# Three pairs of heads per block of products with v, and two feature blocks per bank of turned expert tokens

## The chip, the cores and the metric

The kernel runs on one core of one Trainium2 chip. The metric is the device time of one execution in microseconds (us), the median of several runs. Beside the timed runs one execution was profiled; its rows are what the prediction reads.

## The reference

Three layers follow each other, all in 32-bit floats.

- Attention with talking heads: 4 batches, 12 heads, 448 positions, 64 columns per head. The scores q k^T / 8 of all heads are mixed by a 12 x 12 matrix (w_pre), a softmax over the keys follows, its result is mixed over the heads by a second matrix (w_post), and then multiplied with v.
- A dense layer over the 1792 tokens: x w_in (768 to 2048), ELU, w_out (2048 to 768).
- A layer of 8 experts: each token goes to the expert with the largest gate logit, passes w1 (768 to 1024), ReLU and w2 (1024 to 768), and is scaled by its gate.

## The kernel before

**Attention.** Each batch's 448 query positions are cut into chunks of 120, 120, 120 and 88 (16 chunks, cc = 0 to 15). A chunk is cut into groups of 20 positions (6, 6, 6 and 5 groups), and one group passes through in one slot of a hand-written order. Its steps are:

- `qk` (L222, tile p_qk): scores of one pair of heads for a whole chunk; `qk_out` (L229 on DVE, L231 on ACT) copies them to the scratch tile st.
- `relayout` (L239): DMAs issued by POOL bring one group's 12 heads side by side (tile sp).
- `premix` (L248, p_pre): the first mix over heads; `rowmax` (L253, DVE) takes its extremes, and `expo` (L259, ACT) the exponentials with their sums (tile pt).
- `scale` (L265 to L269, DVE) puts 1/sum into the second mixing matrix; `postmix` (L278, p_post) does the second mix, transposed. Its PSUM tile, two banks, has one buffer (tag "post"). `mt_out` (L296, ACT) copies it to mt, which collects a chunk's groups.
- `av` (L322, p_av): the products with v for some pairs of heads of a whole chunk, into one PSUM bank (tag "av", one buffer); `av_out` (L329, DVE) copies it to xc, and L330, a DMA on SP's queue, writes that to the scratch array xscr.

The order is fixed beforehand: every call is entered by `at(slot, order, fn)` or `half(y, ...)` with y in half slots, and all entries are issued sorted by slot and order number. Each engine's queue works in that order. `S0[cc]` is the slot of chunk cc's first group. Group x has its premix at slot x, its exponentials at x + 1, its postmix at x + 2.5 and its mt_out at x + 3. In an integer slot the order is qk, premix, scale, qk_out (DVE), rowmax, expo (of the group before), mt_out; in a half slot it is qk_out (ACT), av if one is due, postmix. `turns` gives the slots of av. `room` picks, for work that can wait (av_out, and the steps that decode weights), the half slot with the least planned load of an engine.

The last two chunks have all their av blocks at one slot, in several banks.

**Dense layer.** `moe1` starts as attention ends and reads xscr; its code isn't touched.

**Experts.** `moe2` takes the experts in the order PLACES, with 256, 288, 288 and then five times 256 token rows. For each of them 8 "h" jobs (first product, L1218 with tile p_h) are followed by 8 "z" jobs (L1203, p_z, where the rows are a multiple of 128) or 6 "y" jobs (L1218, p_y). The next expert's rows are gathered by DMA (L1165) and turned by `trans(p, ks)` during the z or y jobs of the one before: PE transposes (L90) into a bank p_t (tag "t", two buffers), an ACT copy to the high part xgh (L1181) and a DVE subtraction for the low part xgl (L1182), one feature block of 128 at each of the jobs 0 to 5. The same stretch splits the weights into high and low parts (L110 on ACT, L112 on DVE).

Of the kernel before, what the change touches and what calls it, by code (L numbers as in the profile page):

```python
# [5 lines left out]
F32 = mybir.dt.float32  # L6
# [3 lines left out]
AF = mybir.ActivationFunctionType  # L10
ALU = mybir.AluOpType
# [6 lines left out]
NE, FE = 8, 1024  # L18
NTOK = NB * S
JC, NJ = 112, 4  # L20
KD = DM // 128
# [23 lines left out]
def blocks(n):  # L45
    return [min(128, n - o) for o in range(0, n, 128)]
# [41 lines left out]
def transpose(nc, out, in_, ident):  # L88

    nc.tensor.transpose(out, in_, ident)  # L90
# [10 lines left out]
def after(tc, ins, writes):  # L101
    for w in writes:
        tc.add_manual_dep(ins.ins, w.ins.name, mybir.DependencyInfo(mybir.DependencyClass.Sync, mybir.DependencyReason.DATA),
                          reason="rows of any scatter")
# [42 lines left out]
NCH = NB * 4  # L147
S0 = [0]
# [6 lines left out]
def attention(tc, pools, at, q, k, v, kron_pre, kron_post, dec_jobs, xscr):  # L155
# [3 lines left out]
    nc = tc.nc  # L159
    mm = nc.tensor.matmul  # L160
    sb = pools.open("a_sb", "right")
    early = pools.open("a_early", "left")
    ps = pools.open("a_ps", "right", PSUM)
    ps_qk = pools.open("a_psqk", "left", PSUM)
# [12 lines left out]
    ks, qs, qp, st, sp, pre, mxs, pt, sms, kpt, pst, mt, vt, avp, draw, dsteps = ({} for _ in range(16))  # L177
# [127 lines left out]
    def av(cc, a):  # L305

        n = CHUNKS[cc % 4]
        if cc == NCH - 1:

            p = ps.tile([128, 512], F32, name="p_av", tag="pre", bufs=3)  # L310
        elif cc == NCH - 2 and a:
            if a == 1:
                avp["two"] = [ps_qk.tile([128, 512], F32, name="p_av", tag=f"qk{e}") for e in range(2)]
            p = avp["two"][a - 1]
        else:
            p = ps_qk.tile([128, 512], F32, name="p_av", tag="av")
        p = avp[cc, a] = p[:, :256].rearrange("p (u c) -> p u c", c=128)
        for u in range(2):
            for j in range(4):
                for e in range(2):  # L320
                    h = 4 * a + 2 * u + e
                    mm(p[64 * e:64 * e + 64, u, :n], lhsT=vt[cc // 4][:, j, h, :], rhs=mt[cc][:, j * H + h, :n],  # L322
                       start=(j == 0), stop=(j == 3))

    def av_out(cc, a):
        b, c = divmod(cc, 4)
        n, o = CHUNKS[c], sum(CHUNKS[:c])
        x = sb.tile([128, 2, 120], F32, name="xc", tag="xc", bufs=3)
        nc.vector.tensor_copy(x[:, :, :n], avp.pop((cc, a))[:, :, :n])  # L329
        nc.sync.dma_start(xscr[b][:, 2 * a:2 * a + 2, o:o + n], x[:, :, :n])  # L330

    def dec_load(n, hf):
        draw[n, hf] = dec.load(dec_jobs[n][0], hf)
# [12 lines left out]
    def half(y, order, fn, *args):  # L346
        at(y / 2, order, fn, *args)

    def take(y, **cost):
        for e, c in cost.items():  # L350
            use[e, y] = use.get((e, y), 0) + c
        return y

    def room(lo, hi, **cost):
        return take(min(range(lo, max(lo, hi) + 1), key=lambda y: max(use.get((e, y), 0) + c for e, c in cost.items())), **cost)

    def when(cc, u):

        if cc == 0:
            return 2 * ((2 * u + 1) * 10 // 12 - 13)  # L360
        lo, hi = S0[cc - 1] - 3, S0[cc] - 3
        return 2 * lo + u * (2 * hi - 2 * lo) // 6

    for cc in range(NCH):
        z = S0[cc]
        for u in range(6):
            y = when(cc, u)
# [5 lines left out]
        for g, (T, nr) in enumerate(UNITS[cc % 4]):  # L373
            x = z + g
# [7 lines left out]
            at(x + LAG + 1, 26, mt_out, cc, g)  # L382
            take(2 * x, dve=185, act=200)
            take(2 * x + 1, act=60)
    turns = {(cc, a): 2 * (S0[cc + 1] + (2 if cc >= NCH - 2 else 3 + 2 * a)) + 1 for cc in range(NCH) for a in range(3)}
    for (cc, a), y in turns.items():
        half(y, 9, av, cc, a)
        soon = cc >= NCH - 2 or y + 2 in turns.values()
        half(y if soon else room(y + 1, y + 2, dve=35), 36, av_out, cc, a)
    for b in range(NB):  # L390
        for j in range(4):
            at(S0[4 * b] - 6 + j if b else 1 + j, 4, load_v, b, j)
# [5 lines left out]
    N = 2 * len(dec_jobs)  # L398
    first, free = 3, [0, 0]
    for i in range(N):  # L400
        n, hf = divmod(i, 2)
# [5 lines left out]
        y = room(y + 1, y + 2, act=61)  # L407
        half(y, 36, dec_step, n, hf, 1)
        y = room(y, y + 1, dve=57)
        half(y, 42, dec_step, n, hf, 3)  # L410
        y = room(y + 1, y + 2, dve=101)
# [696 lines left out]
def moe2(tc, pools, w1, w2, ident_d, x2rows, R, out):  # L1108
    nc = tc.nc
    mm = nc.tensor.matmul  # L1110
    P = {}
# [9 lines left out]
    def size(p):  # L1121
        return SIZES[PLACES[p]]
# [12 lines left out]
    def load(n):  # L1135
        if n < NJB:
            p, s, i = jobs[n]
            e = R["of"][PLACES[p]]
            if s == "h":
                t = P["w1"].tile([128, DM], F32, name="w1raw", tag="w1raw", bufs=6)  # L1140
                ins = nc.sync.dma_start(t, w1f[bass.ds(e * (NFE * 128) + i * 128, 128), :])
            elif s == "y":
                t = P["sb"].tile([128, NFE, 128], F32, name="w2raw", tag="w2raw", bufs=5)
                src = w2f[bass.ds(e * FE, FE), i * 128:(i + 1) * 128]
                ins = nc.sync.dma_start(t, src.rearrange("(f p) c -> p f c", p=128))
            else:
                t = P["sb"].tile([128, DM], F32, name="w2raw", tag="w2raw", bufs=5)
                ins = nc.sync.dma_start(t, w2f[bass.ds(e * FE + i * 128, 128), :])
            raws[n] = t
            return ins  # L1150

    def prep(n):
        if n < NJB:
            p, s, i = jobs[n]
            if s == "h":
                ws[n] = split(nc, P["w1"], raws.pop(n), "w1", [128, DM], 3)
            else:
                ws[n] = split(nc, P["sb"], raws.pop(n), "w2", [128, NFE, 128] if s == "y" else [128, DM], 3)

    def gather(p):  # L1160
        bl = blocks(size(p))
        g = xg[p] = P["w1"].tile([128, len(bl), DR], F32, name="xg", tag="xg")
        at = R["tok"][:, PLACES[p]] if p else R["tok1"][:, 0]
        gate[p] = P["w1"].tile([128, len(bl)], F32, name="gate", tag="gate", bufs=2)
        return [nc.gpsimd.indirect_dma_start(g[:n, j, :], None, x2rows, IndirectOffsetOnAxis(at[:n, j:j + 1], 0))  # L1165
                for j, n in enumerate(bl)]

    def trans(p, ks):
        sb = P["sb"]
        N = size(p)  # L1170
        if 0 in ks:
            xgs[p] = (sb.tile([128, KD, N], F32R, name="xgh", tag="xgh"),
                      sb.tile([128, KD, N], F32R, name="xgl", tag="xgl"))
        g, (hi, lo) = xg[p], xgs[p]

        ts = {kk: bank("t") if p == 0 and kk > 1 else P["t"].tile([128, 512], F32, name="p_t", tag="t", bufs=2) for kk in ks}
        for j, n in enumerate(blocks(N)):
            for kk in ks:
                transpose(nc, ts[kk][:, j * 128:j * 128 + n], g[:n, j, kk * 128:(kk + 1) * 128], P["ident"][:n, :n])
        for kk in ks:  # L1180
            nc.scalar.activation(hi[:, kk, :], ts[kk][:, :N], AF.Copy)  # L1181
            nc.vector.tensor_tensor(lo[:, kk, :], ts[kk][:, :N], hi[:, kk, :].bitcast(F32), ALU.subtract)  # L1182
        if KD - 1 in ks:
            for j, n in enumerate(blocks(N)):
                nc.scalar.activation(gate[p][:n, j:j + 1], g[:n, j, DM:], AF.Copy)

    def bank(nm):
        return P["ps"].tile([128, 512], F32, name=f"p_{nm}", tag="y", bufs=4)
# [69 lines left out]
    def rest():  # L1258
        P["sb"] = pools.open("e_sb", "left")
        P["ps"] = pools.open("e_ps", "right", PSUM)  # L1260
        P["sep"] = P["sb"].tile([1, 1], F32, name="sep")
        load(0)
        for n in range(1, 9):

            after(tc, load(n), P["got"][:1] if n == 1 else [])
        prep(0)
        trans(0, range(KD))
        prep(1)
        prep(2)
        for n in range(NJB + 1):  # L1270
            if n < NJB:
                p, s, i = jobs[n]
                if s == "h" and i == 1 and p + 1 < NE:
                    gather(p + 1)
                load(n + 9)
                run(n)
                prep(n + 3)
                if s != "h" and i < KD and p + 1 < NE:
                    trans(p + 1, [i])
            if n >= 1:  # L1280
                finish(n - 1)
        pools.close("e_sb", "e_ps", "e_pst", "e_w1", "m_x2")
# [165 lines left out]
```

## Time and profile before

| | us |
|---|---|
| median of 3 runs | 1209.93 (1209.03 to 1212.42) |
| the profiled execution | 1198.01 |
| its span, from first to last instruction | 1196.2 |
| PE (matmul) busy | 1148.1 |
| DVE busy | 766.2 |
| ACT busy | 683.5 |
| POOL busy | 295.4 |

Busy times are unions of an engine's instructions; ends of matmuls are modelled, so that neighbours overlap in the records and the pace of PE is read from start to start. In the timeline a row is a run of equal instructions of one line: start, duration, engine, line, operation, output and input, shapes, count. In square brackets stands the engine's idle time before it and what ended it. A pair "x2" of records belongs to one product of 32-bit floats, so a block of 16 products shows as x32. Attention fills the span to about 350 us, the dense layer to about 860, the experts the rest.

### The profile page before, as it was taken

To read this page: it belongs to the slowest core of one execution; us is meant where nothing else is said; L and a number is where in the kernel's file an instruction comes from. 1 tells how busy PE (TensorE), PEld (TensorE's weight loads), DVE (VectorE), ACT (ScalarE), POOL (GpSimd) and SP (SyncE) were. 2 spreads that over 40 slices of the span, in tenths; PEclk is the share of its full clock that TensorE was granted. 3 is DMA by queue.
4 is the path that set the end of the run, shared out by engine and by line. 5 is a ranking of instruction groups with operands and counts; after the bars stand their busy time and mean duration, and the time that the engine had idled before them with its cause. 6 is when DMAs were issued, how large, how long until landed. Compare 5 with 4: busy or idle time off the path is not lost.

```text
span 1196.2 us, 31070 instructions
## 1 busy us (share of the span) xinstructions
PE 1148.1 (96%) x12798; PEld 975.4 (82%) x12798; DVE 766.2 (64%) x1540; ACT 683.5 (57%) x1310; POOL 295.4 (25%) x466
## 2 busy tenths in 40 slices
PE   6999999999988999999999999999989999999995
PEld 1566666666667999999999987989779999999995
DVE  2777876777765878677777656555365655566662
ACT  2877876877875674645555344555434544455552
POOL 3765656656630003020211100000010110111110
PEclk7999999999999999999999999999999999999998
DMA  7698698897664528365573623434166665666651
GB/s 207 185 234 202 184 234 205 204 229 198 175 184 131 150 79 219 119 141 136 146 192 100 154 68 100 133 99 141 46 228 209 217 175 190 203 226 230 203 198 63
DMA packets 116444, 201.47 MB, mean 168 GB/s; under 512 B 45024, under 2 KB 76370, under 8 KB 116292
## 3 DMA queue, kind: packets, MB, share of 16 engines
q1 hardware_dynamic: 78116, 138.01, 37.5%
q0 software_dynamic: 38176, 61.37, 21.4%
q8 instruction: 103, 1.69, 0.6%
q14 instruction: 49, 0.40, 0.1%
HBM read 120.94 MB, written 30.09 MB: 126 GB/s over the span
## 4 chain that ended last, share of the span: by engine, by line
PE 88%; ACT 4%; DVE 3%; DMA 2%; issue 1%; POOL 0%; SPq 0%; POOLq 0%; ACTq 0%; DVEq 0%
PE p_h L520 14%; PE p_o L560 14%; PE p_h L1218 11%; PE p_z L1203 8%; PE p_post L278 7%; PE p_av L322 7%; PE p_pre L248 6%; PE p_qk L222 5%; PE acc L586 5%; PE p_o L520 4%; PE p_y L1218 3%; DMA sp<-st 1%; ACT mt L296 1%; PE p_t L90 1%; PE tp L90 1%
## 5 line engine op out<-in xcount | busy, mean ns | idle before, releaser
L239 POOL DMA_DIRECT2D sp<-st x360 | 208.6, 596 | 129.9 <-PE p_pre L248 59.9
L259 ACT ACTIVATE pt<-p_pre,mx 128x448 f32<-128x448 f32 x180 | 112.8, 635 | 43.2 <-DVE mx L253 43.0
L278 PEld LDWEIGHTS p_post<-kp,pt 60*64 60x64 f32 (+1 forms) x5056 | 88.6, 134 | 44.1 <-ACT mt L296 31.1
L253 DVE TENSOR_REDUCE mx<-p_pre 128x1 f32<-128x448 f32 x180 | 104.1, 619 | 27.3 <-PE p_pre L248 22.7
L296 ACT ACTIVATE mt<-p_post 128x960 f32<-128x960 f32 (+1 forms) x92 | 101.7, 1105 | 34.0 <-PE p_post L278 33.8
L278 PE MATMUL p_post<-kp,pt 60*64 60x60 f32 (+2 forms) x5056 | 108.9, 228 | 10.0 <-issue 4.9
L577 POOL DMA_DIRECT2D x<-part x46 | 41.3, 921 | 294.7 <-ACT part L576 291.7
L1218 PE MATMUL p_h<-xgl,w1h 128*128 128x256 f32 (+1 forms) x384 | 109.3, 285 | 0.6 <-DVE xgl L1182 0.5
L1218 PE MATMUL p_h<-xgh,w1l 128*128 128x256 f32 (+1 forms) x384 | 109.3, 285 | 0.3 <-DVE w1l L112 0.3
L248 PE MATMUL p_pre<-sp,kpre 60*64 60x448 f32 x720 | 105.9, 551 | 3.8 <-DMA sp<-st 3.8
L1218 PE MATMUL p_h<-xgh,w1h 128*128 128x256 f32 (+1 forms) x384 | 109.4, 285 | 0.0
L560 PE MATMUL p_o<-gh,woh 128*128 128x448 f32 x288 | 106.4, 370 | 2.6 <-DVE x L573 2.6
L222 PE MATMUL p_qk<-ks,qs 64*64 64x448 f32 x744 | 100.0, 557 | 9.0 <-ACT st L231 5.1
L560 PE MATMUL p_o<-gl,woh 128*128 128x448 f32 x288 | 105.2, 365 | 0.0
L560 PE MATMUL p_o<-gh,wol 128*128 128x448 f32 x288 | 104.9, 364 | 0.0
L322 PEld LDWEIGHTS p_av<-mt,vt 128*64 128x64 f32 x1536 | 74.6, 138 | 31.6 <-DVE kp L269 12.7
L229 DVE COPY st<-p_qk 128x448 f32<-128x448 f32 x93 | 57.9, 622 | 63.1 <-PE p_qk L222 60.1
L112 DVE TENSOR_TENSOR w2l<-w2raw,w2h 128x768 fp32r<-128x768 f32 (+1 forms) x60 | 60.7, 1012 | 51.7 <-ACT w2h L110 51.7
L540 DVE SCALAR_TENSOR_TENSOR th<-rm,th 128x448 f32<-128x448 f32 x64 | 40.0, 625 | 79.8 <-ACT rm L539 79.8
L1254 POOL DMA_INDIRECT out_dram<-yrow,put x18 | 23.8, 1323 | 252.8 <-ACT w1h L110 86.6
L322 PE MATMUL p_av<-mt,vt 128*64 128x120 f32 (+1 forms) x1536 | 84.3, 264 | 0.5 <-ACT mt L296 0.5
L112 DVE TENSOR_TENSOR w1l<-w1raw,w1h 128x768 fp32r<-128x768 f32 x64 | 60.9, 960 | 28.3 <-ACT w1h L110 25.1
(196 smaller groups left out, 2804.3 us busy)
## 6 DMA issues: line engine op xcount, KB each, us to landing
sp<-st POOLq DMA_DIRECT2D x352, 105.0 KB
w1raw<-in_w_dram SPq DMA_DIRECT2D x64, 384.0 KB, 6.9
w2raw<-in_w_dram SPq DMA_DIRECT2D x48, 384.0 KB, 2.9
x<-part POOLq DMA_DIRECT2D x46, 224.0 KB
raw<-in_w_in_dram SPq DMA_DIRECT2D x13, 768.0 KB, 5.7
raw<-in_w_out_dram SPq DMA_DIRECT2D x13, 768.0 KB, 5.2
wtmp<-wscr SPq DMA_DIRECT2D x19, 384.0 KB, 4.0
wtmp<-oscr SPq DMA_DIRECT2D x19, 384.0 KB, 5.2
```

The costliest lines, as they stand in the source:

```text
L112: nc.vector.tensor_tensor(l, src, a.bitcast(F32), ALU.subtract)
L222: mm(p[e][64 * a:64 * a + 64, :S], lhsT=qq[r, c:c + 64], rhs=kk[r], start=True, stop=True)
L239: nc.gpsimd.dma_start(t[64 * r:64 * r + 12 * T, c], st[cc][f:f + d * (T - 1) + 1:d])
L248: mm(ban[r][64 * c:64 * c + 64, :S], lhsT=kpre[x], rhs=t[x, c, :], start=True, stop=True)
L253: nc.vector.tensor_reduce(mxs[cc, g][:, r:r + 1], pre[cc, g][r][:, :S], AX.X, ALU.min)
L259: nc.scalar.activation(pt[cc, g][:, r], pre[cc, g][r][:, :S], AF.Exp, bias=mxs[cc, g][:, r:r + 1], scale=-1.0, accum_out=sms[cc, g][:, r:r ...
L278: mm(out, lhsT=e[x, r, 64 * s:64 * s + 64], rhs=kp[x, w].rearrange("p w (h i) -> p w h i", i=5)[:, :, :, :T], start=True, stop=True)
L296: nc.scalar.activation(dst, src, AF.Copy)
L322: mm(p[64 * e:64 * e + 64, u, :n], lhsT=vt[cc // 4][:, j, h, :], rhs=mt[cc][:, j * H + h, :n], start=(j == 0), stop=(j == 3))
L520: mm(p[:, :S], lhsT=a[:, c], rhs=m, start=(i == 0), stop=(i == 17))
L560: mm(p[:, :S], lhsT=a[:, c], rhs=m, start=(k == 0), stop=(k == 3 * len(fs) - 1))
L1218: mm(q[:, :N], lhsT=a[:, kk, :], rhs=m[:, kk, :], start=(j == 0), stop=(j == len(seq) - 1))
```

## The change

In `av` and `av_out` a block covers three pairs of heads instead of two, so that a chunk has two blocks (a = 0, 1) instead of three. A block is due at S0[cc + 1] + 3.5 + 3a instead of + 3.5 + 2a; for the last two chunks still all at one slot. The tile xc becomes half as wide again and has two buffers instead of three; the planned load of its copy is 50 instead of 35. In `trans` the feature blocks are taken in sets: of two where two times the rows fit into 512 columns, of one otherwise. A set has one bank, one ACT copy and one DVE subtraction, and is made at the first of the two jobs.

```diff
         elif cc == NCH - 2 and a:
-            if a == 1:
-                avp["two"] = [ps_qk.tile([128, 512], F32, name="p_av", tag=f"qk{e}") for e in range(2)]
-            p = avp["two"][a - 1]
+            p = ps_qk.tile([128, 512], F32, name="p_av", tag="qk0")
         else:
             p = ps_qk.tile([128, 512], F32, name="p_av", tag="av")
-        p = avp[cc, a] = p[:, :256].rearrange("p (u c) -> p u c", c=128)
-        for u in range(2):
+        p = avp[cc, a] = p[:, :384].rearrange("p (u c) -> p u c", c=128)
+        for u in range(3):
             for j in range(4):
                 for e in range(2):
-                    h = 4 * a + 2 * u + e
+                    h = 6 * a + 2 * u + e
...
-        x = sb.tile([128, 2, 120], F32, name="xc", tag="xc", bufs=3)
+        x = sb.tile([128, 3, 120], F32, name="xc", tag="xc", bufs=2)
         nc.vector.tensor_copy(x[:, :, :n], avp.pop((cc, a))[:, :, :n])
-        nc.sync.dma_start(xscr[b][:, 2 * a:2 * a + 2, o:o + n], x[:, :, :n])
+        nc.sync.dma_start(xscr[b][:, 3 * a:3 * a + 3, o:o + n], x[:, :, :n])
...
-    turns = {(cc, a): 2 * (S0[cc + 1] + (2 if cc >= NCH - 2 else 3 + 2 * a)) + 1 for cc in range(NCH) for a in range(3)}
+    turns = {(cc, a): 2 * (S0[cc + 1] + (2 if cc >= NCH - 2 else 3 + 3 * a)) + 1 for cc in range(NCH) for a in range(2)}
...
-        half(y if soon else room(y + 1, y + 2, dve=35), 36, av_out, cc, a)
+        half(y if soon else room(y + 1, y + 2, dve=50), 36, av_out, cc, a)
...
+    def width(p):
+        return 2 if p and 2 * size(p) <= 512 else 1
+
     def trans(p, ks):
...
-        ts = {kk: bank("t") if p == 0 and kk > 1 else P["t"].tile([128, 512], F32, name="p_t", tag="t", bufs=2) for kk in ks}
+        w = width(p)
+        sets = [ks[i:i + w] for i in range(0, len(ks), w)]
+        ts = [bank("t") if p == 0 and i > 1 else P["t"].tile([128, 512], F32, name="p_t", tag="t", bufs=2) for i in range(len(sets))]
+        ts = [t[:, :w * N].rearrange("p (k n) -> p k n", k=w) for t in ts]
         for j, n in enumerate(blocks(N)):
-            for kk in ks:
-                transpose(nc, ts[kk][:, j * 128:j * 128 + n], g[:n, j, kk * 128:(kk + 1) * 128], P["ident"][:n, :n])
-        for kk in ks:
-            nc.scalar.activation(hi[:, kk, :], ts[kk][:, :N], AF.Copy)
-            nc.vector.tensor_tensor(lo[:, kk, :], ts[kk][:, :N], hi[:, kk, :].bitcast(F32), ALU.subtract)
+            for t, kks in zip(ts, sets):
+                for i, kk in enumerate(kks):
+                    transpose(nc, t[:, i, j * 128:j * 128 + n], g[:n, j, kk * 128:(kk + 1) * 128], P["ident"][:n, :n])
+        for t, kks in zip(ts, sets):
+            c = slice(kks[0], kks[-1] + 1)
+            nc.scalar.activation(hi[:, c, :], t, AF.Copy)
+            nc.vector.tensor_tensor(lo[:, c, :], t, hi[:, c, :].bitcast(F32), ALU.subtract)
...
-                if s != "h" and i < KD and p + 1 < NE:
-                    trans(p + 1, [i])
+                if s != "h" and i < KD and p + 1 < NE and i % width(p + 1) == 0:
+                    trans(p + 1, range(i, i + width(p + 1)))
```

## Rows read from the trace of the kernel before

**Rows 1.** The page, part 1: busy us, share of the span, instructions
```profile
PE 1148.1 (96%) x12798; PEld 975.4 (82%) x12798; DVE 766.2 (64%) x1540; ACT 683.5 (57%) x1310; POOL 295.4 (25%) x466
```

**Rows 2.** Windows: us, busy of PE, PEld, DVE, ACT, POOL, clock, DMA, GB/s
```profile
54.00:157.00 103.00, 100.31 (x2480) 68.38 (x2476) 75.64 (x202) 79.21 (x172) 62.27 (x108) 1.00 0.83 204
157.00:346.00 189.00, 183.20 (x4530) 124.02 (x4522) 137.48 (x376) 145.35 (x313) 116.30 (x201) 1.00 0.82 204
...
1080.00:1115.00 35.00, 35.00 (x253) 34.81 (x252) 21.50 (x32) 18.27 (x34) 5.58 (x6) 1.00 0.66 221
```

**Rows 3.** Timeline of PE, two slots of attention: start us, duration us, instructions
```profile
172.62 1.18 PE L278 MATMUL p_post<-kp,pt 60*64 60x60 f32 x56
...
174.33 0.98 PE L248 MATMUL p_pre<-sp,kpre 60*64 60x448 f32 x8
175.09 1.16 PE L278 MATMUL p_post<-kp,pt 60*64 60x60 f32 x56
176.00 1.00 PE L222 MATMUL p_qk<-ks,qs 64*64 64x448 f32 x8
176.75 1.09 PE L248 MATMUL p_pre<-sp,kpre 60*64 60x448 f32 x8
177.77 1.86 PE L322 MATMUL p_av<-mt,vt 128*64 128x120 f32 x32
179.56 1.18 PE L278 MATMUL p_post<-kp,pt 60*64 60x60 f32 x56
```

**Rows 4.** Timeline of ACT and DVE in the same two slots
```profile
173.85 1.14 ACT L296 ACTIVATE mt<-p_post 128x960 f32<-128x960 f32 x1 [1.34 <-PE p_post L278]
...
175.37 1.16 DVE L253 TENSOR_REDUCE mx<-p_pre 128x1 f32<-128x448 f32 x2
...
176.09 0.63 ACT L259 ACTIVATE pt<-p_pre,mx 128x448 f32<-128x448 f32 x1 [0.71 <-DVE mx L253]
...
177.32 1.13 ACT L296 ACTIVATE mt<-p_post 128x960 f32<-128x960 f32 x1
```

**Rows 5.** Attention before the first p_av: a window of five slots, and the timeline
```profile
35.90:50.90 15.00, 13.39 (x360) 7.92 (x360) 13.30 (x36) 14.01 (x32) 12.68 (x23) 1.00 0.67 193
...
40.61 1.13 ACT L296 ACTIVATE mt<-p_post 128x960 f32<-128x960 f32 x1
...
41.79 1.18 PE L278 MATMUL p_post<-kp,pt 60*64 60x60 f32 x56 [0.55 <-ACT mt L296]
...
44.93 1.18 PE L278 MATMUL p_post<-kp,pt 60*64 60x60 f32 x56 [0.46 <-ACT mt L296]
```

**Rows 6.** Timeline: a slot with p_pre ahead of p_qk; one after the last scores
```profile
81.89 1.14 PE L278 MATMUL p_post<-kp,pt 60*64 60x60 f32 x56
...
83.81 1.14 ACT L296 ACTIVATE mt<-p_post 128x960 f32<-128x960 f32 x1
...
333.76 1.18 PE L278 MATMUL p_post<-kp,pt 60*64 60x60 f32 x56 [0.47 <-ACT mt L296]
```

**Rows 7.** The chain that ended last: start us, us; three p_av blocks in a row
```profile
346.13 5.14 PE p_av L322 x96
```

**Rows 8.** Experts and copies: the chain, the timeline, and groups by line and form
```profile
1064.45 2.12 PE p_z L1203 x12
1066.79 2.12 PE p_z L1203 x12
...
1076.12 4.20 PE p_z L1203 x24
...
1011.46 0.39 PE L1218 MATMUL p_h<-xgl,w1h 128*128 128x256 f32 x1 [0.47 <-DVE xgl L1182]
...
L329 DVE COPY xc<-p_av 128x240 f32<-128x240 f32 x36 | 14.4, 400 | 3.7 <-PE p_av L322 3.6
...
L1181 ACT ACTIVATE xgh<-p_t 128x256 fp32r<-128x256 f32 x36 | 12.9, 375 | 4.6 <-PE p_t L90 4.6
L1182 DVE TENSOR_TENSOR xgl<-p_t,xgh 128x256 fp32r<-128x256 f32 x36 | 14.6, 419 | 1.2 <-ACT xgh L1181 1.2
```

## The prediction

> **What bounds the kernel now.** I read the page first: TensorE (PE) is busy 96% of the span [rows 1]. Then the windows view: between 54 and 346 us, the regular part of attention, PE is idle 2.7 of 103 us and 5.8 of 189 us, 8.5 us together, and among the experts not at all [rows 2]. So nothing that ACT or DVE are spared can come out of the time unless PE waits for it; what counts is whether PE gets new waits, and what its own work costs.
>
> The two places that the change touches are read in the timeline. [rows 3] are PE's blocks in two slots of attention, each from its start to the next one's. A slot is p_post, p_qk, p_pre; every second one ends with a block of 32 p_av records. Without p_av it is 172.62 to 175.09, 2.47 us. With it: p_post 0.91, p_qk 0.75, p_pre 1.02, p_av 1.79, together 4.47. Two slots are 6.94. Note that p_pre takes 0.75 when p_post follows and 1.02 when p_av does: changing over to p_av costs PE 0.27 us.
>
> The second thing to see is what the next p_post waits for. Its PSUM tile has one buffer, so it needs the ACT copy mt (L296) of the one before. [rows 4] show that copy twice. After the p_post of 172.62 it runs at 173.85 to 174.99, just in time for the p_post of 175.09. After the p_post of 175.09 it is late: p_pre ran at 174.33 to 175.31, so the row maxima start at 175.37, the first exponential at 176.09, a second follows, and ACT, which works in order, reaches mt at 177.32 and ends it at 178.45, 3.36 us after that p_post began. Today this costs nothing: PE is in the p_av block until 179.56. **The p_av block of every second slot hides a late mt.**
>
> **Part 1: p_av in two blocks per chunk.** The 24 products of three pairs go into one bank (384 of its 512 columns). Products, bytes and packets stay as they are; blocks fall from 48 to 32, with as many DVE copies and SP DMAs.
>
> The due slots matter. Chunk cc has its blocks 3.5 and 6.5 slots after the next chunk's first group, where it had them 3.5, 5.5 and 7.5 after. Chunks have 6, 6, 6 and 5 groups, so for chunks 0 to 13 the blocks stand at 28 slots (9.5, 12.5, 15.5 ... 84.5, 87.5) with 27 gaps: 24 of three slots and 3 of two. Today 41 gaps: 38 of two, 3 of one. **In each gap of three there are two slots in a row without p_av**, a case that [rows 3] don't have.
>
> Price of such a gap. Call the p_post after a block A, the next ones B and C. A to B is 2.47 as today. B to C: everything that decides mt's lateness lies ahead of the block that is taken away, so mt still ends 3.36 after B, and p_post starts some 0.05 later (mt 40.61 to 41.74, p_post 41.79 [rows 5]): 3.41 where 2.47 would do, a wait of 0.94. C to the next A: 0.91 + 0.75 + 1.02 and the larger block. Three blocks in a row, 96 records, took 5.14 [rows 7], so 48 take 2.57 by that and 2.69 as 1.5 times 1.79; I take the middle, 2.63: 5.31. Three slots are 2.47 + 3.41 + 5.31 = 11.19, where today's pace gives 1.5 x 6.94 = 10.41: 0.78 more, the fewer changeovers already taken off (they and the joint block are worth 0.16 to 0.2 a gap).
>
> The trace has a stretch to check it: before slot 9 there are no p_av blocks. There five slots took 15.0 us, 3.0 each, two of them 6.0 against my 5.88, with PE idle 0.55 and 0.46 ahead of p_post for mt [rows 5]. So the wait is real, and comes about once in two slots.
>
> Of the 24 gaps, 3 lie where a five-group chunk turns the order of p_qk and p_pre round. There mt ends earlier: 81.89 to 84.95, 3.06 [rows 6]; against 2.41 of work it is a wait of 0.70, net 0.54. One more lies after the last scores, where PE already waits 0.47 for mt in slots without p_av [rows 6]; I take nothing for it. Sum: 20 x 0.78 + 3 x 0.54 = 17.2 us.
>
> Against this, other waits can shrink: the transfers, ACT and the scratch for the next chunk gain 0.78 us in each three slots. All of PE's other idle time there is 8.5 us [rows 2], which bounds it: between 0 and 8.5. I take 4, since some of it is seen as late ACT and DMA work and some only as issue. **Attention: +13.**
>
> Costed at nothing: the DVE copy L329, 0.40 us for 240 columns [rows 8], which would be some 0.5 for 360 (estimate, a quarter more for half as many columns again) but comes once in three slots instead of once in two; it stands behind the row maxima of its half slot and has three slots until the bank is wanted. Without that cover it would cost 0.1 us 32 times, 3 us. The xc tile has two buffers for three, against copies half again as far apart. The last read of mt comes one slot earlier. SP issues 16 DMAs fewer, and nothing queued behind them is late. Chunks 14 and 15 keep their blocks back to back at the same slot, as now.
>
> **Part 2: expert tokens.** Where two feature blocks fit a bank (256 tokens: five of the eight experts' transfers), 30 pairs of ACT copy and DVE subtraction become 15 of 512 columns. They cost 0.375 and 0.419 us now [rows 8], beside a PE that is busy all 35 us of such an expert [rows 2]: nothing to gain from them, and nothing to lose while an even step (2.34 us) holds a weight split and one larger pair. The transposes keep their number. A step with two takes 2.34 us, without 2.10 (4.20 for two [rows 8]): 0.24. How much of this belongs to the pair and how much to changing over isn't shown; the bounds are nothing and half of it, 15 x 0.12 = 1.8. I take 1.4. The last pair is made one step earlier, which removes the 0.47 us wait on xgl at 1011.46 [rows 8], 0.6 with its restart. **Experts: -2.**
>
> **Sum.** The profiled execution has 1198.0 us (span 1196.2); 17.2 - 4 - 2 = +11 makes it 1209. The median of the runs shown, 1209.93, lies 1% above it, and I put the difference on that: **1221 us**.
>
> **Rivals.**
> Faster: mt isn't late for C. The decision point is 2.41 us after B, when PE could start p_post; mt would have to end there and not at 3.36. For it: ACT has 0.71 us of idle time ahead of those exponentials, and DVE's other work is moved a little. Against: the chain from p_pre over row maximum and two exponentials is already tight (0.06, 0.1 us between its links [rows 4]), and [rows 5] show it late without p_av too. Price: 14 changeovers at 0.27 and some 1.5 of joint blocks, -5, experts -2: 1203. The Trainium skill (TensorEngine Tiling (Array Packing), Key Properties) says that changing the tiling mode drains TensorE, so fewer p_av blocks among 64-row products should mean fewer drains; the 0.27 of [rows 3] agrees, and by that rule alone the time would fall to about this rival's.
> No change: the new waits swallow all the idle time of today: 17.2 - 8.5 - 2 = +7 with my price; with the waits at the recorded 0.5 of [rows 5] less 0.16 instead of 0.78, 24 x 0.34 - 4 - 2 = +2: 1212.
> Slower still: nothing shrinks and the load works (decode steps on ACT, the larger copy on DVE) fall into slot C, where anything on ACT's queue ahead of mt now delays PE: 17.2 + 3 = +20: 1230.
>
> **Chances.** Forecast 0.62; slower still 0.20; no change 0.11; faster 0.07. About 0.3%, 3.6 us, is what a measurement of this kernel can tell from no change. Of the forecast's and the heavier case nearly all lies beyond it: slower 0.83, same 0.10, faster 0.07. The range 1211 to 1230 runs from the no-change case's edge to the heavier one; only the faster rival and some tails stay out.
>
> **What would show it.** Right: in the changed profile p_av blocks of 48 records three slots apart (10.4 us becomes about 11.2); ahead of every third p_post an idle PE that ends on ACT mt, together 15 to 20 us; the sum of p_av's records smaller; no new idle PE among the experts, and the wait at xgl gone. Wrong: 10.4 us from block to block with no wait on mt, or waits on p_av's bank, xc or the transposes' banks.

## The result and the profile after

The changed kernel takes 1222.37 us (median of 6 runs, 1215.92 to 1226.67); the kernel before took 1207.05 us beside it (median of 6 runs, 1202.35 to 1212.42). The ratio is 1.0135, with an interval of 1.0102 to 1.0167: slower by 15.3 us. The profiled execution took 1222.1 us, with a span of 1220.3, and stands at the median; the profiled execution of before, 1198.0, was shorter than every other run of that kernel in this study, so the two spans alone would give 24 us, and more profiles are needed for a fair account (below).

The page of the changed kernel, part 1, columns as in [rows 1]:

```profile
PE 1151.0 (94%) x12798; PEld 981.0 (80%) x12798; DVE 763.5 (63%) x1509; ACT 681.4 (56%) x1295; POOL 294.5 (24%) x466
```

PE has as many instructions and 3 us more of busy time; the span has grown by 24. The new time is idle time of PE. The windows say where (columns as in [rows 2]; the second window ends at the last p_av blocks, the third is one expert):

```profile
54.00:157.00 103.00, 91.92 (x2216) 63.44 (x2212) 68.18 (x180) 71.44 (x155) 56.10 (x99) 0.98 0.75 185
157.00:372.00 215.00, 196.08 (x4790) 134.56 (x4792) 144.23 (x386) 153.50 (x332) 122.32 (x212) 0.98 0.76 189
1098.00:1133.00 35.00, 35.00 (x256) 34.90 (x255) 21.18 (x29) 17.98 (x32) 5.55 (x6) 1.00 0.66 224
```

Attention has 11.1 and 18.9 us of idle PE, 30.0 together, for 8.5 in [rows 2]. The expert has none, as before. One more number differs: the granted clock, 0.98 for 1.00.

**The slots.** The timeline of PE in one gap of three slots, from the p_post after a p_av block (A) over B and C to the next A:

```profile
139.82 1.18 PE L278 MATMUL p_post<-kp,pt 60*64 60x60 f32 x56
...
141.53 0.98 PE L248 MATMUL p_pre<-sp,kpre 60*64 60x448 f32 x8
142.28 1.14 PE L278 MATMUL p_post<-kp,pt 60*64 60x60 f32 x56
143.19 0.98 PE L222 MATMUL p_qk<-ks,qs 64*64 64x448 f32 x8
143.95 1.09 PE L248 MATMUL p_pre<-sp,kpre 60*64 60x448 f32 x8
145.69 1.18 PE L278 MATMUL p_post<-kp,pt 60*64 60x60 f32 x56 [0.66 <-ACT mt L296]
146.65 0.98 PE L222 MATMUL p_qk<-ks,qs 64*64 64x448 f32 x8
147.41 0.97 PE L248 MATMUL p_pre<-sp,kpre 60*64 60x448 f32 x8
148.31 2.68 PE L320 MATMUL p_av<-mt,vt 128*64 128x120 f32 x48
150.92 1.18 PE L278 MATMUL p_post<-kp,pt 60*64 60x60 f32 x56
```

A to B is 2.46, B to C 3.41 (p_pre stands 1.74 ahead of C, where it takes 0.75 ahead of B), C to the next A 5.23: 11.10 in all, and the gaps like it that have no other wait repeat that to 0.03 (10.46, where the block that ends the gap is one of an 88-column chunk). The timeline of ACT in the same gap:

```profile
141.04 1.14 ACT L296 ACTIVATE mt<-p_post 128x960 f32<-128x960 f32 x1 [1.01 <-PE p_post L278]
...
143.28 0.63 ACT L259 ACTIVATE pt<-p_pre,mx 128x448 f32<-128x448 f32 x1 [0.71 <-DVE mx L253]
...
144.52 1.13 ACT L296 ACTIVATE mt<-p_post 128x960 f32<-128x960 f32 x1
```

It is the picture of [rows 4], instruction for instruction: behind B the row maxima, two exponentials, then mt, which ends at 145.65, 3.37 after B. What has changed is PE alone: no p_av block stands there any more, and PE waits. The chain of waits in the same stretch (start us, us, what) runs where it ran over PE before:

```profile
143.28 1.34 ACT pt L259 x4
144.62 1.03 ACT mt L296
...
145.69 1.18 PE p_post L278 x49
```

**PE's waits on "issue".** The waits of PE from 25 to 375 us (total us, times, longest):

```profile
PE p_post L278 <- ACT mt L296: 10.8, 18, 0.7
PE p_post L278 <- issue: 8.8, 6, 2.5
PE p_qk L222 <- issue: 8.2, 3, 3.5
```

In before the first line had 4.8 us, and issue 4.9 in all. So the largest new item under these names isn't the wait that was forecast: 17.0 us end on nothing that the profile names. (The names tell less than the pace. Of the 0.95 that a late C costs, 0.66 is named; the rest stands in the records as a longer p_pre, for the ends of matmuls are modelled.) The longest waits on issue, in the chain of waits of the changed kernel:

```profile
111.76 2.45 issue
...
193.74 2.94 issue
...
284.87 3.49 issue
```

One of them by windows of the changed kernel (busy of PE first, the last three columns are the granted clock, the DMA engines' share and GB/s):

```profile
186.00:190.00 4.00, 4.00 (x93) 3.14 (x89) 2.84 (x10) 2.54 (x6) 1.19 (x2) 1.00 1.01 249
...
194.00:196.70 2.70, 0.02 (x3) 0.03 (x3) 0.35 (x2) 1.27 (x3) 1.18 (x3) 0.85 0.81 218
196.70:198.30 1.60, 1.60 (x11) 0.75 (x14) 0.00 (x0) 0.54 (x1) 0.00 (x0) 0.50 0.91 235
198.30:200.00 1.70, 1.70 (x30) 1.18 (x24) 1.28 (x3) 0.07 (x1) 0.00 (x0) 0.50 1.04 243
```

The DMA engines are full, PE stands still for 2.7, and then its clock is granted at 0.50, which is 1.2 of 2.4 GHz; it is back at full speed some 6 us after the standstill. This happens three times in the profile (at about 114, 196 and 288 us), each time behind one of the long waits above. It isn't in [rows 2], where the clock is 1.00.

**Experts and copies.** The groups by line and form (out<-in xcount | busy us, mean ns | idle before), which answer to [rows 8]:

```profile
L327 DVE COPY xc<-p_av 128x360 f32<-128x360 f32 x24 | 12.5, 522 | 4.2 <-DMA xscr<-xc 2.6 <-PE p_av L320 1.6
...
L1188 DVE TENSOR_TENSOR xgl<-p_t,xgh 128x512 fp32r<-128x512 f32 x15 | 10.3, 685 | 0.0
L1187 ACT ACTIVATE xgh<-p_t 128x512 fp32r<-128x512 f32 x15 | 8.7, 583 | 0.0
```

And the chain of waits through one expert:

```profile
1069.86 16.90 PE p_h L1224 x144
1086.75 2.09 PE p_z L1209 x12
1088.84 0.44 PE p_t L90 x4
1089.28 4.17 PE p_z L1209 x24
...
1104.74 5.28 PE p_h L1224 x45
```

From one p_h to the next it is 34.88 us; in before the same distance was 35.06 (1045.25 to 1080.31). The wait of p_h on xgl [rows 8] is gone. From the first p_h to the last p_z the experts take 296.78 us for 298.16.

### The profile page after: what moved, and what is told of

Its sections match the earlier page's. It is cut to its first block, busy times and chain, and to the rows that moved or that the text cites. A ratio compares the mean times of both kernels' runs of the same rounds, so it can differ in the third digit from the quotient of the medians.

```text
span 1220.3 us, 30980 instructions
## 1 busy us (share of the span) xinstructions
PE 1151.0 (94%) x12798; PEld 981.0 (80%) x12798; DVE 763.5 (63%) x1509; ACT 681.4 (56%) x1295; POOL 294.5 (24%) x466
## 4 chain that ended last, share of the span: by engine, by line
PE 84%; ACT 6%; DVE 4%; DMA 3%; issue 2%; POOL 1%; SPq 0%; ACTq 0%; POOLq 0%; DVEq 0%
PE p_h L518 14%; PE p_o L558 13%; PE p_h L1224 12%; PE p_z L1209 8%; PE p_av L320 7%; PE p_post L278 6%; PE p_qk L222 5%; PE acc L584 5%; PE p_pre L248 5%; PE p_o L518 4%; PE p_y L1224 3%; DMA sp<-st 2%; ACT mt L296 2%; ACT pt L259 2%; DVE mx L253 1%
## 5 line engine op out<-in xcount | busy, mean ns | idle before, releaser
L278 PEld LDWEIGHTS p_post<-kp,pt 60*64 60x64 f32 (+1 forms) x5056 | 92.6, 135 | 67.8 <-ACT mt L296 50.0
L278 PE MATMUL p_post<-kp,pt 60*64 60x60 f32 (+2 forms) x5056 | 112.5, 229 | 24.1 <-ACT mt L296 11.8
L222 PE MATMUL p_qk<-ks,qs 64*64 64x448 f32 x744 | 106.1, 568 | 15.3 <-issue 8.2
L320 PE MATMUL p_av<-mt,vt 128*64 128x120 f32 (+1 forms) x1536 | 81.5, 263 | 0.7 <-ACT mt L296 0.7
L489 ACT ACTIVATE gh<-th 128x448 fp32r<-128x448 f32 x64 | 37.0, 578 | 71.8 <-DVE th L539 71.8
```

The source lines that it names most:

```text
L222: mm(p[e][64 * a:64 * a + 64, :S], lhsT=qq[r, c:c + 64], rhs=kk[r], start=True, stop=True)
L278: mm(out, lhsT=e[x, r, 64 * s:64 * s + 64], rhs=kp[x, w].rearrange("p w (h i) -> p w h i", i=5)[:, :, :, :T], start=True, stop=True)
```

## The experiments

**The two parts alone.** Theory: all of the loss comes from the p_av blocks, and the experts give back a little. Part 1 alone puts back the transposes and copies of before:

```diff
-        w = width(p)
-        sets = [ks[i:i + w] for i in range(0, len(ks), w)]
...
+            nc.scalar.activation(hi[:, kk, :], ts[kk][:, :N], AF.Copy)
+            nc.vector.tensor_tensor(lo[:, kk, :], ts[kk][:, :N], hi[:, kk, :].bitcast(F32), ALU.subtract)
```

> Part 1 alone: p_av in two blocks per chunk, the expert tokens turned as before. Theory (a late mt in every gap of three slots): the slower time stays, some 15 us over the kernel before, ratio 1.012 to 1.016; p_post to p_post goes 2.46, 3.41, 5.2 us; the experts take as long as before, and the 0.47 us wait on xgl is there again. Rival (the two parts add up differently, the experts lose): at most 5 us over the kernel before.

Part 2 alone puts back three blocks of two pairs:

```diff
-        for u in range(3):
+        for u in range(2):
...
-                    h = 6 * a + 2 * u + e
+                    h = 4 * a + 2 * u + e
...
-    turns = {(cc, a): 2 * (S0[cc + 1] + (2 if cc >= NCH - 2 else 3 + 3 * a)) + 1 for cc in range(NCH) for a in range(2)}
+    turns = {(cc, a): 2 * (S0[cc + 1] + (2 if cc >= NCH - 2 else 3 + 2 * a)) + 1 for cc in range(NCH) for a in range(3)}
```

> Part 2 alone: expert tokens in sets of two, p_av as before. Theory: nothing waits for the copies, only transposes and the one wait on xgl give a little: 1 to 2 us less from the end of attention to the end of the program, ratio 0.998 to 1.000, in the total hardly to be told from no change; attention as before, 2.46 and 4.47 us from p_post to p_post. Rival (a share of the slowdown comes from the experts): over 1.003.

Measured, both beside 1204.76 us of before: part 1 alone 1219.33 us, ratio 1.0111 (1.0089 to 1.0133); part 2 alone 1205.42 us, ratio 0.9993 (0.9967 to 1.002). The loss is part 1's. Part 2's gain is too small for the whole time to show it, and is read from the trace: first p_h to last p_z 297.01 us, 1.2 less than before, and in the seven profiles of this study with part 2 and all loads it is 296.6 to 297.2, for 298.0 to 298.7 in the four without part 2.

**Gaps of two and four slots.** If a gap of three costs because its second slot without p_av comes late, the loss should depend on how the slots are dealt out. The second block of a chunk is made due one slot earlier:

```diff
-... else 3 + 3 * a)) + 1 for cc in range(NCH) for a in range(2)}
+... else 3 + 2 * a)) + 1 for cc in range(NCH) for a in range(2)}
```

> The changed kernel with its two blocks per chunk due 3.5 and 5.5 slots after the next chunk's first group, in place of 3.5 and 6.5: gaps of two and four slots by turns, the same blocks. Theory (the wait belongs to the second slot in a row without p_av, and the next one has none, as in the stretch before the first block): no wait in a gap of two, 0.94 us and some 0.2 in a gap of four, so about 0.75 us a chunk less than the changed kernel: some 9 us less, ratio to the kernel before near 1.005. Rival 1 (the size of a block costs, not its place): as the changed kernel, 1.013. Rival 2 (each slot without p_av after the first waits 0.94): 1.013 as well, with a second late slot in every gap of four.

Measured: 1216.62 us, ratio 1.0091 (1.0063 to 1.0118). The timeline of PE in a gap of four slots of this kernel:

```profile
163.13 1.13 PE L278 MATMUL p_post<-kp,pt 60*64 60x60 f32 x56
...
166.54 1.18 PE L278 MATMUL p_post<-kp,pt 60*64 60x60 f32 x56 [0.65 <-ACT mt L296]
...
169.18 1.18 PE L278 MATMUL p_post<-kp,pt 60*64 60x60 f32 x56
```

One slot of 3.41, and the next is 2.64 again: a late mt lets ACT catch up. This gap pays once, like a gap of three, and a gap of two pays nothing. But only four of the ten gaps of four are like it; in the other six the slot after the late one takes 3.0 to 3.9 as well. So the waits weren't halved: 17 slots without p_av have an mt that ends more than 2.95 us after its p_post, for 24, 22 and 23 in the three profiles of the same blocks in gaps of three. Six fewer at 0.69 to 0.95 are 4 to 6 us, and by the ratios about 5 us came back. The expected 9 us didn't, the issue waits remained (11.2 us, one of them 4.60), and the clock fell twice. The direction and the count of late slots speak for the theory.

**Where the wait is made: the late mt on another engine.** In the groups whose mt is late the copy goes to DVE, with scale, row maximum and av_out moved out of its way:

```diff
-        nc.scalar.activation(dst, src, AF.Copy)
+        if S0[cc] + g in late:
+            nc.vector.tensor_copy(dst, src)
+        else:
+            nc.scalar.activation(dst, src, AF.Copy)
...
-            at(x + LAG + 1, 26, mt_out, cc, g)
+            at(*((x + LAG + .5, 11) if x in late else (x + LAG + 1, 26)), mt_out, cc, g)
```

> The changed kernel, but the copy mt of the second group after each block, the one that comes late on ACT behind two exponentials, is made by DVE right after its p_post; in these gaps the scaling of the next group and the copy of p_av are moved out of its way. Theory (the wait is on that copy and its place on ACT alone): mt ends some 2.5 to 2.8 us after its p_post in place of 3.36, p_post to p_post becomes about 2.5 to 2.9 in place of 3.41, 24 times, 12 to 20 us less than the changed kernel: ratio to the kernel before 0.997 to 1.003. Rival 1 (ACT and DVE together are the bound in three slots): the wait only moves to the row maxima or the exponentials, within 5 us of the changed kernel. Rival 2 (PE's waits on issue are what the change added): they stay, 8 us or more over the kernel before.

Measured: 1219.46 us, ratio 1.0104 (1.0082 to 1.0126), which can't be told from the changed kernel's 1.0135. The timeline of this kernel, a gap whose B stood at 149.56:

```profile
151.30 1.19 DVE L297 COPY mt<-p_post 128x960 f32<-128x960 f32 x1
...
152.55 1.18 PE L278 MATMUL p_post<-kp,pt 60*64 60x60 f32 x56
...
153.97 1.15 DVE L253 TENSOR_REDUCE mx<-p_pre 128x1 f32<-128x448 f32 x2
...
154.68 0.63 ACT L259 ACTIVATE pt<-p_pre,mx 128x448 f32<-128x448 f32 x1 [1.95 <-DVE mx L253]
...
155.46 0.98 PE L248 MATMUL p_pre<-sp,kpre 60*64 60x448 f32 x6 [0.29 <-ACT pt L259]
```

C comes 2.99 after B for 3.41, so the place is right. But the row maxima now stand behind mt on DVE, ACT waits 1.95 for them, and the next p_pre waits for the exponentials: what one slot saves the next one loses, and the 12 to 20 us of the theory didn't come.

**The same on ACT, by order.** mt goes ahead of the two exponentials instead of behind them:

```diff
-            at(x + LAG + 1, 26, mt_out, cc, g)
+            at(x + LAG + 1, 23 if x in late else 26, mt_out, cc, g)
```

> The changed kernel with ACT's order turned round in the 24 slots with a late mt: mt ahead of the two exponentials. Theory (mt is late because two exponentials are before it, but these are wanted too: p_pre of the next slot needs their PSUM bank): mt ends some 2.4 us after its p_post, but the next p_pre waits for the exponential, so PE's wait moves there; within 5 us of the changed kernel. Rival (the place of mt alone costs the time): p_post to p_post back to 2.5, 15 to 22 us less, ratio to the kernel before 0.995 to 1.001.

Measured: 1221.24 to 1231.35 us in three runs, ratio 1.0123 (1.005 to 1.0197): no gain. The timeline, B at 253.04:

```profile
254.22 1.13 ACT L296 ACTIVATE mt<-p_post 128x960 f32<-128x960 f32 x1 [0.90 <-PE p_post L278]
...
255.97 0.60 PE L248 MATMUL p_pre<-sp,kpre 60*64 60x448 f32 x3 [0.35 <-ACT pt L259]
```

mt ends 2.31 after B, in time. Now p_pre waits: for exponentials 10.0 us in 19 waits, and only 2.7 us for mt. The exponentials and the copy don't fit in 2.47 us on ACT behind those row maxima, in either order; the p_av block was the room that they had.

**More work ahead of mt, with and without the cover.** The second exponential of the group is run twice, into the same tile, ahead of every mt in question. By the traces that is 21 times in the changed kernel (201 exponentials for 180) and 35 times in before (215 for 180), not 24 and 38: in three of those slots the group is a short one that has only one exponential.

```diff
-        nc.scalar.activation(pt[cc, g][:, r], pre[cc, g][r][:, :S], AF.Exp, bias=mxs[cc, g][:, r:r + 1], scale=-1.0,
-                             accum_out=sms[cc, g][:, r:r + 1])
+        for _ in range(2 if r and S0[cc] + g in twice else 1):
+            nc.scalar.activation(pt[cc, g][:, r], pre[cc, g][r][:, :S], AF.Exp, bias=mxs[cc, g][:, r:r + 1], scale=-1.0,
+                                 accum_out=sms[cc, g][:, r:r + 1])
```

> The changed kernel with one ACT instruction more ahead of each late mt: in the 24 groups whose exponentials stand on ACT's queue before it, the second exponential is done twice, with the same result; 0.61 us more each. Theory (PE waits for mt there, nothing covers it): p_post to p_post goes from 3.41 to some 4.0, 24 x 0.61 = 14.6, so 10 to 15 us over the changed kernel; ratio to the kernel before 1.020 to 1.026. Rival (the wait is put down to mt, but PE really waits for something else): within 3 us of the changed kernel.

> The kernel before with the same extra exponential ahead of mt in each slot that ends with p_av: 38 times, 23 us more work for ACT. Theory (the p_av block covers a late mt): mt ends 3.97 us after its p_post in place of 3.36, the next p_post starts 4.47 after it anyhow; 0 to 4 us more, ratio 1.000 to 1.004. Rival (ACT's total work is the bound in attention): some 20 us more, ratio 1.015.

Measured, beside 1207.48 us of before: changed kernel 1226.99 us, ratio 1.015 (1.0096 to 1.0204); before 1205.63 us, ratio 0.9982 (0.9953 to 1.0011). The timeline of PE in the changed kernel with the extra work:

```profile
234.20 1.13 PE L279 MATMUL p_post<-kp,pt 60*64 60x60 f32 x56
...
238.37 1.18 PE L279 MATMUL p_post<-kp,pt 60*64 60x60 f32 x56 [1.42 <-ACT mt L297]
```

and of before with it:

```profile
237.10 1.14 PE L279 MATMUL p_post<-kp,pt 60*64 60x60 f32 x56
...
239.73 1.86 PE L323 MATMUL p_av<-mt,vt 128*64 128x120 f32 x32
...
240.04 1.13 ACT L297 ACTIVATE mt<-p_post 128x960 f32<-128x960 f32 x1
...
241.52 0.60 PEld L279 LDWEIGHTS p_post<-kp,pt 60*64 60x64 f32 x34 [0.16 <-issue]
```

This is the clearest pair. In before mt now ends 4.07 after B, and PE loses nothing, for it is in p_av until 241.52: some 23 us of added ACT work (35 exponentials; ACT is busy 706.3 us for 683.5) cost no time. In the changed kernel the same 0.6 us moves C from 3.41 to 4.17. That the cover is what the change takes away is shown. In the whole time it came to some 2 us by the ratios (1.015 for 1.0135) and 5 by the medians, under the 10 to 15 that were expected and under 21 x 0.76 = 16: by the whole time alone the rival, within 3 us, isn't ruled out. The trace is what tells. PE's waits on mt are 18.5 us there for 10.8. From the first p_av block to the joined last ones it takes 321.4 us, 7.4 more than the mean of the three profiles below, with 3.7 less of issue waits and 1.6 less lost to the clock, so some 13 of the 16 are there. Where PE stands for another reason in the same gap, the longer wait is partly hidden: a gap with 1.57 us of issue wait took 12.5 (from 94.31), where one without takes 11.86.

**How steady are the issue waits?** Each kernel is profiled a second time, unchanged.

> The kernel before, unchanged, profiled a second time: for PE's waits on issue in attention, 4.9 us in the first profile of it, 11.2 with the same attention in the run with part 2 alone, 17.0 in the changed kernel. Theory (they differ from execution to execution): 5 to 12 us here. Rival (the change adds them, and 11.2 was rare): near 5.

> The changed kernel, unchanged, profiled a second time: PE's waits on issue in attention were 17.0 us in its first profile and 11.1 to 13.9 in five runs with blocks of three pairs, against 4.9 to 11.2 in four with blocks of two. Theory (a few us more with the change, the rest differs from execution to execution): 10 to 15 us here. Rival (17.0 belongs to the changed kernel): 16 or more.

Measured: before 1203.47 us with 8.3 us of PE's waits on issue (25 to 375 us), changed 1222.3 us with 13.4. Now there are four profiles with blocks of two pairs (before twice, part 2 alone, the doubled exponential in before) and three with blocks of three that change nothing else (the changed kernel twice, part 1 alone):

| | two pairs | three pairs | difference |
|---|---|---|---|
| first p_av block to the joined last ones, us | 291.7, 295.2, 300.6, 301.0: mean 297.1 | 317.4, 314.2, 310.4: mean 314.0 | +16.9 |
| PE's waits on issue from 25 to 375 us | 4.9, 8.3, 11.2, 10.7: mean 8.8 | 17.0, 13.4, 13.9: mean 14.8 | +6.0 |
| lost to the clock in the stretch of the first row, us (estimate: PE's busy time by one less the granted clock, in windows of 2 us) | 0, 0, 0, 0 | 6.1, 5.8, 3.2: mean 5.0 | +5.0 |

16.9 less 1.5 of the experts is 15.4, and the medians differ by 15.3. So this sample stands for the runs, though the profiles of one group differ by 7 to 9 us.

**Whose are the issue waits?** They fall where SP issues loads of v among others and the DMA engines are full. In both kernels the v loads of batches 1 to 3 are left out, and the first batch's v is used throughout:

```diff
-        vt[b] = sb.tile([128, 4, H, D], F32, name="vt", tag="vt", bufs=2)
+        vt[b] = vt[0] if b else sb.tile([128, 4, H, D], F32, name="vt", tag="vt", bufs=2)
...
+        if b:
+            return
```

> The changed kernel without the loads of v for the batches 1 to 3 (it multiplies with the first batch's v all along), so that 5 MB less comes in during attention. Theory (PE's long waits on issue come where the loads of v fill the DMA engines): the waits of 1.7 us and more near 100, 112, 194 and 285 us go, PE's waits on issue in attention fall from 13 to 17 us to 6 or less; the waits on mt stay at 3.41 us from p_post to p_post. Rival (the waits on issue have to do with the blocks of 48): 11 us or more still.

> The kernel before without the same loads of v. Theory: its waits on issue fall as well, from 5 to 11 us to 4 or less, and the difference between the two kernels without these loads is that of the waits on mt less the experts' gain: 10 to 14 us. Rival: no change in the waits on issue, and the difference stays at 15 us or more.

The whole times, 1462.11 and 1448.71 us, say nothing here: with other values of v the tokens go to other experts, more of them than an expert has places, and work for the overflow runs at the end. Only attention can be read. Windows from the first p_av block to the joined last ones, the changed kernel without those loads:

```profile
54.80:360.60 305.80, 282.57 (x7002) 193.99 (x6998) 211.50 (x565) 223.46 (x485) 178.19 (x309) 0.99 0.71 179
```

and before without them:

```profile
53.10:345.10 292.00, 282.23 (x7000) 192.20 (x6996) 212.86 (x578) 224.28 (x484) 178.00 (x309) 0.99 0.75 189
```

305.8 for 314.0, and 292.0 for 297.1. The issue waits fall to 8.7 and 5.2 us, over the 6 and 4 that were expected and under the 11 of the changed kernel's rival; the loss to the clock is 1.5 and 1.6 (one stretch in each). So by one profile of each kernel some four tenths of the issue waits hang on the v loads in both, and most of the clock's falls in the changed one. With that taken out the change costs 13.8 us in attention, 3.5 of it issue. B to C is still 3.41.

## Why the prediction was right, and where it was not

**The mechanism** was as predicted. The p_av block of every second slot hid a late mt; a gap of three slots leaves one mt uncovered; the block goes from 10.41 to 11.10 us where 11.19 was said. A to B was said to be 2.47 (2.46), B to C 3.41 (3.41), C to A 5.31 (5.23), p_av of 48 records 2.63 (2.61). The 0.08 too much lies in C to A: ahead of p_av the p_pre takes 0.90 here (147.41 to 148.31), where [rows 3] gave 1.02, so changing over costs 0.15 and not 0.27. A usual gap so costs 0.69 over today's pace, for 0.78. But today's pace isn't 10.41 everywhere. A gap with the order turned round, 269.60 to 280.58, took 10.98; two such slots of before take 7.38 and not 6.94 (79.43 to 86.81), which with half a usual pair, 3.47, makes 10.85, so the price there is 0.13 and not 0.54. And in three of the 20 gaps that were priced like the others the exponentials ahead of the late mt are those of the short group, one for two: mt ends 2.77 after B, C comes after 2.82, and the gap takes 10.46 (200.98 to 211.44 in the changed kernel's second profile), where two such slots of before take 6.83 (276.89 to 283.72 in before's second), with 3.47 more 10.30: 0.16. So the gross price is 17 x 0.69 + 3 x 0.13 + 3 x 0.16 = 12.6 us, for 17.2. The Trainium skill (TensorEngine Tiling (Array Packing), Key Properties) says that a change of the tiling mode drains TensorE. The 0.15 agrees with that, and the fewer changes are in the 11.10; by that rule alone the kernel would be faster, and the 0.94 of B to C outweighs it.

**The step that failed** is "Against this, other waits can shrink ... I take 4". It made one term of things that went different ways:

- Waits that shrink. The three-pair blocks pay only 16.9 - 6.0 - 5.0 = 5.9 us beyond issue and clock, 6.7 less than the 12.6 of undisturbed gaps. The waits of p_qk on ACT st fell from 2.8 and 2.2 to 0.6 and 0.3 us, 2 of it. The other 4.7 aren't traced, and with three and four profiles that differ by 7 to 9 us among themselves they may be chance. They aren't gaps in which an issue wait takes the place of the wait on mt: six of nine such gaps in the first profile name no wait on mt, but they last nearly as long as an undisturbed gap and the issue wait together (95.39 to 108.17 is 12.78, for 11.10 + 1.77).
- Issue waits were put among those that can only shrink. They grew by 6.0 us; what they are stands below.
- The clock wasn't in the sum at all. It read 1.00 in [rows 2], and was taken for granted. In the changed kernel it falls to half two or three times: 5.0 us.

So attention had 12.6 - 6.7 + 6.0 + 5.0 = 16.9 where the prediction had 17.2 - 4 = 13. The forecast of 1221.0 is 1.4 from the median of 1222.37 in part by luck: the gaps cost 4.6 less than their price, two items that weren't in the sum cost 11.0, and it put +11 on a median of 1209.93, where six runs gave 15.3 on 1207.05.

**The experts** were said to give 2 and gave 1.5. The 0.6 of the xgl wait came whole: the stage behind it went from 36.22 to 35.33, 0.7 more than the others gained. The transposes' changing over was mis-sized: an expert gains 0.18 us by three pairs fewer, 0.06 a pair for the 0.09 taken, 15 of them about 0.9 for 1.4. **The copies** cost nothing, as said: 0.52 us for 360 columns as estimated; its two xc buffers do bring a wait of 2.6 us on the scratch DMA, which is DVE's and reaches nobody on the path.

**The rivals.** Faster needed mt to end 2.41 after B; it ended 3.37. No change needed the new waits to be swallowed by the old idle time: some of that happened, and the room was filled again by issue and clock. Slower still took decode steps in slot C for its mechanism, with nothing shrinking; the measured +15.3 lies between its +20 and the forecast's +11, by other causes. The sign on the page to look for was given as waits on mt of 15 to 20 us: they show 10.8, of which before had 4.8 already; that sign was mis-sized, for the profile names only 0.66 of each late C, and none where the order is turned round, nor in most gaps with an issue wait.

**What PE waits for when the profile names nothing.** The records answer it. Count PE's records in the trace in order of start, matmuls, weight loads and the sequencer's together. The records that end the issue waits over 0.3 us in the changed kernel are numbers (from 0) 1474, 2241, 2498, 3265, 3778, 6338, 6593, 7362 and 11457: from each to the next it is a multiple of 256, to within one record. So it is with all 97 such waits in attention in the thirteen profiles of this study, in either kernel. And the page lists a queue of instructions (queue and kind: packets, MB, share):

```profile
q8 instruction: 103, 1.69, 0.6%
```

These are 103 packets of 16 KB for 25859 records, one for about 256. Each of the 97 waits ends 1.2 to 1.9 us after such a packet has come in. The one of the standstill from 193.74 moves from 194.29 to 195.41, and PE goes on at 196.68; the DMA view from 194.2 to 195.5 shows it:

```profile
q8 instruction: 1, 0.02, 5.4%
```

So these are late fetches of PE's own instructions, which move on the same DMA engines as the loads.

**Open.** Why they cost more with blocks of three pairs is shown in part. For record 7362 the packet starts 4.5 to 4.7 us after PE has passed the record 256 before it in the three profiles with blocks of three, and 1.4 to 4.5 in the four with blocks of two; for 11457 it is 4.0 to 5.2 and 1.4 to 3.9; for 7618 it is the other way round, 2.4 to 2.9 and 2.4 to 5.3. So the change shifts which fetch falls into the busy stretches. What holds a packet back there, other than the loads of v, isn't shown, and no run moved the fetches alone. Nor is it shown why the clock falls behind some standstills and not behind others.

No version of the change beat before. Part 2 alone is the only one that isn't slower, and it can't be told from before.

## What to carry to other kernels

A block of matmuls that looks like plain work may be the cover of a late copy: before blocks are merged or spread, look in each slot at what the next PSUM tile with one buffer waits for, and when that copy ends beside the block. If it ends behind the place where the block stood, the merged version pays that distance once for each slot uncovered, and to give ACT more work in the old kernel at just that place shows beforehand whether it is covered. New idle time of PE isn't the whole bill: long standstills can bring the clock down behind them, so read the granted clock by windows as well as the waits. And where an engine waits for nothing that the profile names, count its records from one such wait to the next: equal distances, here multiples of 256, point to its instructions, and the packets of the instruction queue tell whether they came late.

## What was not expected of the hardware

TensorE's granted clock went from 1.00 to 0.50 behind standstills of PE in attention, and stayed there for some 3 to 7 us: behind the waits of 111.76, 193.74 and 284.87 in the changed kernel, and two or three times in each of the six other profiles of kernels with three-pair blocks and all loads. In the four profiles with two-pair blocks and all loads it didn't happen before the joined last blocks; without the loads of v it did once (at 166 us), and at the change to the dense layer it falls in every profile (in before at 375). The loss is 3.2 to 6.1 us in a run, as much as the standstills' own growth. One wait's length doesn't decide it: in the profile of part 1 alone the clock fell behind waits of 1.90 and 1.89 us and not behind one of 2.94; in that of the doubled exponential in before it stayed at 1.00 behind one of 2.11.

PE's instructions come in by packets of 16 KB on the DMA engines, and PE stands still when one is late: 97 waits of 0.3 to 4.6 us in thirteen profiles, all at multiples of 256 records (worked out above). These waits differ by several us between executions of one and the same kernel (4.9 and 8.3 in before, 17.0 and 13.4 in the changed one). The kernel before is spread over 1198.0 to 1216.8 us in its runs, and among PE's waits in its two profiles these are the ones that differ most.
